# A Fourier branch associated the other way, with seven products in both stages, under an attention on one core

## The chip, the cores and the metric

The kernel runs on one core of a Trainium2 chip. The metric is the time of one execution on the device in microseconds. A core has TensorE (matrix products, PE in the profile, with its weight loads as PEld), VectorE (DVE), ScalarE (ACT), GpSimd (POOL) and SyncE (SP), which here issues all transfers from one queue, in order. Each engine works off its own list of instructions in order and waits for others by semaphores.

## What is computed

Two independent branches, whose results stand side by side in the output (2048 rows, 1024 + 1024 columns). All data are float32.

```
# A: attention, 2048 rows, width 1024, 32 heads of 32, one shared key and value head
q = x @ wq;  k = x @ wk;  v = x @ wv
p = softmax(q k^T * 32**-0.5);  a = (p v) @ wo
# B: Fourier mixing of another x (2048 x 1024)
a_ = x @ hid_re^T;  b_ = x @ hid_im^T         # hid: 1024 x 1024
y  = seq_re @ a_ - seq_im @ b_                # seq: 2048 x 2048
out = concat([a, y], axis=-1)
```

## The kernel before

**Precision.** TensorE multiplies in the type fp32r, which keeps fewer bits than float32. So each operand tile is split into a high part (`hi`, a cast to fp32r) and a low part (`lo`, the tile less its high part), and one product of tiles is three matmuls: high x high, high x low, low x high.

**Fills.** All large products (queries, keys and values, both stages of the Fourier branch, the output projection) are written as a list of *groups*. A group makes one 128 x 512 tile of a result in one PSUM bank (`psb`): 8 right tiles of 128 x 512, 2 left tiles that hold four 128 x 128 blocks each, 24 matmuls. One such matmul is called a *fill* here, and `take(n)` puts the next n of the list into TensorE's order. At the end of a group its `post` moves the bank to SBUF and on to DRAM.

**Right and left tiles.** Two lines of preparation, `RL` and `ML`, bring each tile through four steps: `load` (SyncE, into one of three staging buffers), `comb` (GpSimd adds or subtracts a second source, where a tile is a sum), `hi` (a cast, on ScalarE in the first 120 fills, on DVE after that) and `lo` (a subtraction on DVE). A step is put into the program when the position in the list of fills is within a *lead* of the item's due position (`RL`: 40, 40, 14, 8 fills; `ML`: 52, 36, 27, 21). The finished pairs stay in rings (`rp` of 14, `mp` of 4), and a step `hi` waits in the program until the tile that it replaces has had its last use. Partial results come back through `yp` (4 buffers). In the names of the profile, `r` and `m` are staging tiles, `rh`, `rl`, `mh`, `ml` the high and low parts, `y` the partial results, `qh` an evicted tile.

**Attention.** 32 units (4 blocks of 512 queries x 8 groups of four heads). For each unit there are 32 score steps and 32 exponential steps. A score step makes two matmuls (`pss<-kst,qst`), DVE takes the row maximum over 1024 keys (`nm`, TENSOR_REDUCE) and ScalarE the exponential with its row sums (`pss<-pss,nm`). These sums give the normalisation of the softmax, in a few small DVE operations per unit (`lse_1`, `lse_2`, names `mm`, `md`, `l`, `m`) and one transpose (`lse_3`). An exponential step, 44 steps later, makes the transposed scores (two matmuls, `pst`) and ScalarE their exponential into `p`. After every second chunk of 128 keys, `pv` multiplies the probabilities with v: a burst of 16 matmuls of 32 columns each (`psb<-p,v`, four heads side by side), whose result DVE adds to `ov`.

**The order** is written out by hand. A prologue of 44 score steps puts 7 fills behind each; then 1024 steps follow, each with one score step and one exponential step, and `level` spreads the fills that are left: none in the step in which a burst stands, the rest evenly over the three other steps of a block of four. `aside` keeps bursts and transposes six fills away from the edges of a group, so that its PSUM bank has been emptied.

**The Fourier branch** uses `PRODUCTS`, a scheme with seven products of half-size blocks for a two by two block product. Before, stage 1 makes x times the four blocks (real and imaginary part, two column halves) of the hidden matrix in 64 groups, and GpSimd forms the sums of these that the scheme needs. Stage 2 multiplies with the sequence matrices by the seven products: 112 groups, since the contraction of 1024 is cut into two halves that meet in `hs` (ScalarE copies the first half, DVE adds the second). Results of products are added up in DRAM through `y`.

Of the kernel before, what the change touches and what calls it, by code (L numbers as in the profile page):

```python
# [8 lines left out]
F32 = mybir.dt.float32  # L9
# [7 lines left out]
P = 128  # L17
# [3 lines left out]
DH = 32  # L21
# [47 lines left out]
def tile_kernel(ctx: ExitStack, tc, xT, wq, wkv, wo, xbT, wT, cT, out):  # L69
# [19 lines left out]
    xb_d = [[[dram.tile([P, 4, P], F32, name=f"xb_{s}_{q}_{a}") for a in range(2)] for q in range(2)] for s in range(NC)]  # L89
# [14 lines left out]
    NR0, NM0, NY = 3, 3, 4  # L104
    NR, NM = 14, 4
# [5 lines left out]
    op = pool(ctx, "op", 2, side="right")  # L111
    hp = pool(ctx, "hp", 1, side="right")
# [107 lines left out]
    RL = Line(NR0, NR, (40, 40, 14, 8), load_r, nothing, hi_r, lo)  # L220
# [106 lines left out]
    qp = pool(ctx, "qp", 1)  # L327

# [3 lines left out]
    def kv_post(b):  # L332
        cols = slice(b * W, (b + 1) * W)

        def post(ps):
            kv = qp.tile([2 * DH, W], F32, name="kv")
            act.activation(kv, ps[:2 * DH], AF.Copy)
            dve.tensor_copy(kst[0:DH, cols], kv[0:DH])
            kl = qp.tile([DH, W], F32R, name="kl")
# [38 lines left out]
    NAMES = {}  # L378
    for _, nt, _ in PRODUCTS:
        key = tuple(nt)  # L380
        NAMES[key] = [dram.tile([P, W], F32, name=f"r{len(NAMES)}_{s}") for s in range(NC)]

    def stage1():
        seen = []
        for r, e in ((0, 0), (1, 1), (0, 1), (1, 0)):
            ws = [Item([(lambda c=c, r=r, e=e: wT[r, e, c], 1)]) for c in range(ND)]
            sg = -1 if r else 1
            todo = [k for k in NAMES if len(k) == 2 and all(t[:2] in seen + [(r, e)] for t in k)
                    and any(t[:2] == (r, e) for t in k)]
            seen.append((r, e))  # L390
            for s in range(NC):
                if len(seen) > 1:
                    left = [Item(None, pre=lambda q=q, s=s: xb_d[s][q]) for q in range(2)]
                else:
                    left = [Item([(lambda q=q, s=s: xbT[s, :, q * 4:(q + 1) * 4], 1)], save=xb_d[s][q]) for q in range(2)]
                ys = []
                for k in todo:
                    o = next(t for t in k if t[:2] != (r, e))
                    ys.append(Item([(lambda o=o, s=s: single(o[:2])[s], 1)]))

                def post(ps, r=r, e=e, s=s, sg=sg, ys=ys, todo=todo):
                    o = op.tile([P, W], F32, name="qh")
                    act.activation(o, ps, AF.Copy, scale=float(sg))
                    sp.dma_start(single((r, e))[s], o)
                    ready.add((((r, e, 1),), s))
                    for k, y in zip(todo, ys):
                        mine = next(t[2] for t in k if t[:2] == (r, e))
                        other = next(t[2] for t in k if t[:2] != (r, e))
                        if other > 0:
                            (gp.tensor_add if mine > 0 else gp.tensor_sub)(y.y, y.y, o)  # L410
                        else:
                            gp.tensor_sub(y.y, o, y.y)
                        sp.dma_start(NAMES[k][s], y.y)
                        ready.add((k, s))
                yield Group(left, ws, post, ys=ys)

    singles = {}

    def single(k):
        if k not in singles:  # L420
            key = ((k[0], k[1], 1),)
            singles[k] = NAMES[key] if key in NAMES else [dram.tile([P, W], F32, name=f"n{k[0]}{k[1]}_{s}") for s in range(NC)]
        return singles[k]

    for r in range(2):
        for e in range(2):
            single((r, e))

    hs = {}

    def right_of(k, s):
        assert (k, s) in ready
        return NAMES[k][s]

    def stage2():
        seen, total = {}, {}
        for _, _, outs in PRODUCTS:
            for t, e, _ in outs:
                total[t, e] = total.get((t, e), 0) + 1
        for mt, nt, outs in PRODUCTS[1:] + PRODUCTS[:1]:  # L440
            for half in range(2):
                R = [Item([(lambda s=s, nt=nt: right_of(tuple(nt), s), 1)]) for s in range(half * 8, half * 8 + 8)]
                for k in range(8):
                    left = []
                    for q in range(2):
                        s0 = half * 8 + q * 4
                        left.append(Item([(lambda a=a, k=k, s0=s0: cT[a[0], a[1] * 8 + k, :, s0:s0 + 4], a[2]) for a in mt]))
                    if half == 0:
                        def post(ps, k=k):
                            hs[k] = hp.tile([P, W], F32, name=f"h{k}")  # L450
                            act.activation(hs[k], ps, AF.Copy)
                        yield Group(left, R, post)
                        continue
                    ys = []
                    plan = []
                    for t, e, sg in outs:
                        n = seen.get((t, e, k), 0)
                        seen[t, e, k] = n + 1
                        it = None
                        if n:  # L460
                            it = Item([(lambda t=t, e=e, k=k: y_d[t][e][k], 1)])
                            ys.append(it)
                        r0 = (t * 8 + k) * P
                        to = out[r0:r0 + P, D + e * W:D + (e + 1) * W] if n + 1 == total[t, e] else y_d[t][e][k]
                        plan.append((sg, it, to))

                    def post(ps, k=k, plan=plan):
                        h = hs[k]
                        dve.tensor_add(h, h, ps)
                        for sg, it, to in plan:  # L470
                            if it is not None:
                                (gp.tensor_add if sg > 0 else gp.tensor_sub)(it.y, it.y, h)
                                sp.dma_start(to, it.y)
                            elif sg > 0:
                                sp.dma_start(to, h)
                            else:
                                o = op.tile([P, W], F32, name="qh")
                                act.activation(o, h, AF.Copy, scale=-1.0)
                                sp.dma_start(to, o)
                    yield Group(left, R, post, ys=ys)  # L480
# [286 lines left out]
```

## Time and profile before

| | us |
|---|---|
| median of 3 runs | 2922.26 (2920.36 to 2922.76) |
| span of the profiled execution | 2920.7 |
| TensorE busy | 2870.4 (98%) |
| DVE busy | 2078.9 (71%) |
| ScalarE busy | 2295.2 (79%) |
| GpSimd busy | 465.0 (16%) |
| transfers | 485.05 MB, mean 166 GB/s |

Busy times are unions of the instructions of an engine. Matmuls overlap in the pipeline, so a TensorE that is always busy may still have gaps between starts. In a row for a group of instructions stand, after the shapes and the count, the busy time in us and the mean duration in ns, and behind the second bar the idle time of the engine before them and what ended it. In a row in order of time stand the start and the duration in us. `L50` is the line of the helper class that records all operations, so the names of the tiles tell the operations apart.

### The profile page before, as it was taken

How to read it: one execution, taken by the hardware profiler on the slowest of the kernel's cores; microseconds unless marked ns; L12 is line 12 of the kernel's file. 1: busy time of each engine (PE TensorE's matmuls, PEld its weight loads, DVE VectorE, ACT ScalarE, POOL GpSimd, SP SyncE). 2: the span in 40 equal slices, each digit the busy share in tenths (PEclk: the TensorE clock that was granted, in tenths of full speed). 3: DMA queues.
4: the chain of work that ended last, by engine and by line, in shares of the span. 5: the costliest groups of instructions: out<-in, count | busy, mean ns of one | idle time of the engine just before them, and what ended most of it. 6: DMA issues, size and time to landing. Idle time of an engine off the chain costs nothing.

```text
span 2920.7 us, 40174 instructions
## 1 busy us (share of the span) xinstructions
PE 2870.4 (98%) x14096; PEld 1943.3 (67%) x14096; DVE 2078.9 (71%) x2721; ACT 2295.2 (79%) x3342; POOL 465.0 (16%) x342
## 2 busy tenths in 40 slices
PE   7999999999999999999999999999999999999999
PEld 4776666666666666666666666666666666666666
DVE  6866777655665656888888888788888888866511
ACT  4688888888888887888888888878878888888751
POOL 0000000011112222322233230023232220110000
PEclk9999999999999999999999999999999999999999
DMA  8865455555666666444455463254454442454446
GB/s 279 298 192 171 157 184 172 167 170 185 192 222 216 205 219 220 148 142 147 129 163 170 120 188 116 76 180 141 144 151 134 148 131 80 146 162 136 124 143 178
DMA packets 318027, 485.05 MB, mean 166 GB/s; under 512 B 33664, under 2 KB 98688, under 8 KB 317824
## 3 DMA queue, kind: packets, MB, share of 16 engines
q1 hardware_dynamic: 317824, 482.48, 52.7%
q8 instruction: 111, 1.82, 0.3%
q14 instruction: 92, 0.75, 0.1%
HBM read 351.54 MB, written 129.76 MB: 165 GB/s over the span
## 4 chain that ended last, share of the span: by engine, by line
PE 89%; DVE 4%; ACT 3%; DMA 2%; issue 2%; POOL 0%; SPq 0%; ACTq 0%; POOLq 0%; DVEq 0%
PE psb L50 56%; PE pss L50 16%; PE pst L50 16%; ACT p L50 2%; DVE nm L50 1%; DVE ov L50 1%; DVE rl L50 1%; DVE ml L50 1%; ACT pss L50 0%; DMA ql<-ql 0%; DMA p<-in_xT_dram 0%; DMA r<-in_xT_dram 0%; DVE mh L50 0%; SPq L50 0%; DVE rh L50 0%
## 5 line engine op out<-in xcount | busy, mean ns | idle before, releaser
L50 DVE TENSOR_REDUCE nm<-pss 128x1 f32<-128x1024 f32 x1024 | 1251.0, 1222 | 372.1 <-PE pss L50 366.3
L50 ACT ACTIVATE p<-pst 128x1024 f32<-128x1024 f32 x1024 | 1051.7, 1027 | 407.2 <-PE pst L50 403.4
L50 ACT ACTIVATE pss<-pss,nm 128x1024 f32<-128x1024 f32 x1024 | 1113.8, 1088 | 93.0 <-DVE nm L50 90.6
L50 PE MATMUL psb<-rh,mh 128*128 128x512 f32 (+1 forms) x1916 | 755.3, 394 | 9.6 <-ACT rh L50 6.7
L50 PE MATMUL psb<-rh,ml 128*128 128x512 f32 (+1 forms) x1916 | 755.2, 394 | 0.5 <-DVE ml L50 0.5
L50 PE MATMUL psb<-rl,mh 128*128 128x512 f32 (+1 forms) x1916 | 754.4, 394 | 0.0
L50 PE MATMUL pss<-kst,qst 128*128 128x512 f32 x2048 | 669.4, 408 | 6.9 <-ACT pss L50 6.5
L50 PE MATMUL pst<-qst,kst 128*128 128x512 f32 x2048 | 656.3, 401 | 15.5 <-ACT p L50 15.4
L50 PEld LDWEIGHTS pss<-kst,qst 128*128 128x128 f32 x2048 | 364.3, 188 | 285.2 <-ACT p L50 114.0
L50 PE MATMUL psb<-p,v 128*32 128x512 f32 x4096 | 492.5, 598 | 0.0
L50 PEld LDWEIGHTS pst<-qst,kst 128*128 128x128 f32 x2048 | 373.0, 188 | 141.8 <-ACT p L50 58.5
L50 PEld LDWEIGHTS psb<-rh,mh 128*128 128x128 f32 (+1 forms) x1916 | 359.2, 187 | 96.3 <-ACT rh L50 7.3
L50 PEld LDWEIGHTS psb<-rh,ml 128*128 128x128 f32 (+1 forms) x1916 | 359.2, 187 | 86.8 <-DVE ml L50 1.6
L50 PEld LDWEIGHTS psb<-rl,mh 128*128 128x128 f32 (+1 forms) x1916 | 359.3, 188 | 86.1 <-issue 1.0
L50 DVE TENSOR_TENSOR ov<-ov,psb 128x512 f32<-128x512 f32 x224 | 154.0, 688 | 321.9 <-PE psb L50 321.5
L50 POOL TENSOR_TENSOR m<-m,m 128x512 f32<-128x512 f32 x160 | 216.6, 1360 | 462.7 <-DMA m<-in_cT_dram 352.6
L50 PEld LDWEIGHTS psb<-p,v 128*32 128x32 f32 x4096 | 106.8, 109 | 245.4 <-issue 220.9
L50 ACT ACTIVATION_READ_ACCUMULATOR pss<-pss,nm 128x1 f32 x1024 | 209.7, 205 | 0.0
L50 DVE TENSOR_TENSOR ml<-m,mh 128x512 fp32r<-128x512 f32 (+1 forms) x274 | 202.3, 739 | 4.2 <-ACT mh L50 3.5
L50 POOL TENSOR_TENSOR y<-y,h 128x512 f32<-128x512 f32 x64 | 88.8, 1398 | 564.7 <-DVE h L50 480.3
L50 DVE TENSOR_TENSOR rl<-r,rh 128x512 fp32r<-128x512 f32 x200 | 150.3, 753 | 5.2 <-ACT rh L50 3.9
L50 POOL MEMSET qst<- 32x2048 f32 x32 | 58.5, 1832 | 578.8 <-PE pst L50 547.3
(63 smaller groups left out, 783.6 us busy)
## 6 DMA issues: line engine op xcount, KB each, us to landing
m<-in_cT_dram SPq DMA_DIRECT2D x384, 256.0 KB, 3.7
r<-r SPq DMA_DIRECT2D x112, 256.0 KB, 3.7
mh<-xb SPq DMA_DIRECT2D x96, 256.0 KB, 3.9
ml<-xb SPq DMA_DIRECT2D x96, 256.0 KB, 4.1
y<-y SPq DMA_DIRECT2D x96, 256.0 KB, 2.9
y<-r SPq DMA_DIRECT2D x80, 256.0 KB, 3.1
r<-y SPq DMA_DIRECT2D x80, 256.0 KB, 2.0
qst<-qh SPq DMA_DIRECT2D x64, 256.0 KB, 5.7
```

The lines of the kernel that those rows point to most:

```text
L50: return lambda *a, **k: self.tc.keep_in_program_order(f(*a, **k))
```

## The change

The Fourier branch is associated the other way: stage A multiplies the sequence matrices with x, stage B the result with the hidden matrices. In both, the seven products of `PRODUCTS` are used with a contraction of 1024, so each product tile is one group: stage A has 7 x 2 (real, imaginary) x 2 (column halves of the sequence block) x 4 = 112 groups, stage B 7 x 2 x 4 = 56. The halves and `hs` go.

Stage A takes x in another layout (`xn_d`). It is made in the prologue: `load_x` loads a tile, `turn_x` transposes four 128 x 128 blocks on TensorE per score step (steps 4 to 35), ScalarE copies them out of PSUM, SyncE stores them.

Right tiles can now be sums of two sources too (`load_r` and `comb` on `RL`). The low parts are made on GpSimd after the first 120 fills. Evictions of both stages are on DVE (`evict`), the additions into partial results on GpSimd (`gather`). The tiles of the sequence matrices and the intermediate results are read in pieces of 512 bytes.

The bursts of `pv` take four chunks of 128 keys instead of two: half as many, twice as long, one in eight steps; `level` spreads the fills over the other seven. Buffers: `NY` 3 instead of 4, `NR` 13 instead of 14, `NM` 10 instead of 4, `op` 3 instead of 2, `pp` 5 instead of 4; `hp` and `qp` go. The leads of `RL` are 44, 32, 22, 12. Twenty tiles, not 24, are loaded ahead of everything.

```diff
-    NR0, NM0, NY = 3, 3, 4
-    NR, NM = 14, 4
+    NR0, NM0, NY = 3, 3, 3
+    NR, NM = 13, 10
...
     def load_r(it):
         if it.pre or it.t:
             return
-        it.t = [r0p.tile([P, W], F32, name="r0")]
-        sp.dma_start(it.t[0], it.srcs[0][0]())
+        it.t = []
+        for n, (ap, _) in enumerate(it.srcs):
+            it.t.append(r0p.tile([P, W], F32, name=f"r{n}", bufs=NR0 - n))
+            a = ap()
+            t = it.t[-1]
+            sp.dma_start(t.rearrange("p (a b) -> p a b", a=a.shape[1]) if len(a.shape) == 3 else t, a)
...
     def lo(it):
         if not it.pre:
-            dve.tensor_sub(it.lo, it.t[0], it.hi.bitcast(F32))
+            (dve if pos["fill"] < START else gp).tensor_sub(it.lo, it.t[0], it.hi.bitcast(F32))
...
-    RL = Line(NR0, NR, (40, 40, 14, 8), load_r, nothing, hi_r, lo)
+    RL = Line(NR0, NR, (44, 32, 22, 12), load_r, comb, hi_r, lo)
...
+    ORDER_A, ORDER_B = (2, 4, 1, 5, 0, 3, 6), (0, 4, 1, 2, 3, 5, 6)
...
+    def gather(plan, h):
+        for sg, it, to in plan:
+            if it is None:
+                assert sg > 0
+                sp.dma_start(to, h)
+            else:
+                (gp.tensor_add if sg > 0 else gp.tensor_sub)(it.y, it.y, h)
+                sp.dma_start(to, it.y)
+
+    def evict(ps, sg=1):
+        h = op.tile([P, W], F32, name="qh")
+        if sg > 0:
+            dve.tensor_copy(h, ps)
+        else:
+            dve.tensor_scalar_mul(h, ps, -1.0)
+        return h
+
+    def c_tile(r, c, t):
+        return cT[r, t * 4:t * 4 + 4, :, c].rearrange("t p c -> p t c")
+
+    def stage_a():
+        seen = {}
+        for at, bt, outs in (PRODUCTS[p] for p in ORDER_A):
+            left = [[Item([(lambda i=i, k=k, m=m, q=q: xn_d[i][m][k * 2 + q], sg) for k, i, sg in at]) for q in range(2)]
+                    for m in range(4)]
+            for r in range(2):
+                for t in range(2):
+                    R = [Item([(lambda k=k, j=j, r=r, t=t, c=c: c_tile(r, k * 8 + c, j * 2 + t), sg) for k, j, sg in bt])
+                         for c in range(8)]
+                    for m in range(4):
...
+                        def post(ps, r=r, plan=plan):
+                            gather(plan, evict(ps, -1 if r else 1))
+                        yield Group(left[m], R, post, ys=ys)
...
+    def stage_b():
+        seen = {}
+        for at, bt, outs in (PRODUCTS[p] for p in ORDER_B):
+            R = [Item([(lambda k=k, j=j, c=c: wT[c // 4, j, k * 4 + c % 4], sg) for k, j, sg in bt]) for c in range(8)]
+            for t in range(2):
+                for m in range(4):
                     left = []
+                    for r in range(2):
+                        left.append(Item([(lambda i=i, k=k, r=r, t=t, m=m: gd[k][i][r][t][:, :, m * P:(m + 1) * P].rearrange("i p c -> p i c"), sg)
+                                          for k, i, sg in at]))
...
+                    def post(ps, plan=plan):
+                        gather(plan, evict(ps))
                     yield Group(left, R, post, ys=ys)
...
-    pp = pool(ctx, "pp", 4)
+    pp = pool(ctx, "pp", 5)
...
-        for c in (2 * k, 2 * k + 1):
+        for c in range(4 * k, 4 * k + 4):
             for h in range(4):
-                te.matmul(ps[h * DH:(h + 1) * DH], v[:, c], pt[u, c][:, h], start=c == 2 * k, stop=c == 2 * k + 1)
+                te.matmul(ps[h * DH:(h + 1) * DH], v[:, c], pt[u, c][:, h], start=c == 4 * k, stop=c == 4 * k + 3)
...
+    def turn_x(n, q):
+        i, m = divmod(n, 4)
+        aside()
+        ps = bank("psb")
+        for c in range(4):
+            te.transpose(ps[:, c * P:(c + 1) * P], xt[n][:, q, c * P:(c + 1) * P], ident)
+        o = op.tile([P, W], F32, name="qh")
+        act.activation(o, ps, AF.Copy)
+        cur["at"] += 1
+        sp.dma_start(xn_d[i][m][q], o.rearrange("p (a b) -> p a b", a=4))
+
     for s in range(SU + LEAD):
         score_step(s)
+        if s % 4 == 0 and s < 32:
+            load_x(s // 4)
+        if 4 <= s < 36:
+            turn_x(*divmod(s - 4, 4))
         take(7)
...
-        x = (n // 4 + max(n % 4 - 1, 0) / 3) / (total // 4)
+        x = (n // 8 + max(n % 8 - 1, 0) / 7) / (total // 8)
...
-        if r % 4 == 0 and n:
-            pv(*divmod(n // 4 - 1, 8))
+        if r % 8 == 0 and n:
+            pv(*divmod(n // 8 - 1, 4))
```

More of the change, by code (lines that the diff above doesn't have):

```diff
@@ L375, in q_group @@
         return Group(left, xs, post)
[L378 to L436, printed above, removed]
-        for _, _, outs in PRODUCTS:
[L438 to L443, printed above, removed]
-                    left = []
[L445 to L458, printed above, removed]
@@ new lines, in tile_kernel, with totals @@
+    ORDER_A, ORDER_B = (2, 4, 1, 5, 0, 3, 6), (0, 4, 1, 2, 3, 5, 6)
+    def totals():
+        total = {}
+        for _, _, outs in PRODUCTS:
+            for i, j, _ in outs:
+                total[i, j] = total.get((i, j), 0) + 1
+        return total
+    def gather(plan, h):
[6 more added lines that the diff above has]
+                sp.dma_start(to, it.y)
```

68 lines of the change are left out of this document (38 added, 30 removed).

## Prediction

> **What bounds the kernel now.** I read the page first (busy shares, then the chain), then the table by stretches, then the order of time of a few microseconds in the middle, and last the groups.
>
> ```profile
> span 2920.7 us, 40174 instructions
> ...
> PE 2870.4 (98%) x14096; PEld 1943.3 (67%) x14096; DVE 2078.9 (71%) x2721; ACT 2295.2 (79%) x3342; POOL 465.0 (16%) x342
> ...
> PE 89%; DVE 4%; ACT 3%; DMA 2%; issue 2%; POOL 0%; SPq 0%; ACTq 0%; POOLq 0%; DVEq 0%
> ```
>
> TensorE is busy for 98% and makes 89% of the chain. A busy TensorE is not yet a full one, so I look at the stretches: prologue, query products, the two spectral stages, the output products. The columns are PE, PEld, DVE, ACT, POOL busy, the clock, the DMA share and GB/s.
>
> ```profile
> 120.00:165.00 45.00, 44.96 (x195) 35.83 (x193) 36.23 (x50) 29.17 (x50) 0.00 (x0) 1.00 0.82 271
> 165.00:600.00 435.00, 432.64 (x2151) 292.10 (x2151) 305.07 (x396) 366.33 (x538) 11.09 (x7) 1.00 0.53 171
> 600.00:1100.00 500.00, 496.28 (x2468) 334.80 (x2467) 300.93 (x348) 418.43 (x614) 93.64 (x71) 1.00 0.63 203
> 1100.00:2100.00 1000.00, 987.04 (x4890) 662.70 (x4888) 818.16 (x1091) 819.29 (x1189) 240.50 (x175) 1.00 0.48 148
> ```
>
> TensorE idles for 13 us of 1000 where DVE is 82% busy, for 2.4 of 435 where DVE is 70% busy. The granted clock is 1.00. What one matmul costs is the distance of starts, not its 0.39 us:
>
> ```profile
> 1502.35 0.40 PE L50 MATMUL psb<-rh,ml 128*128 128x512 f32 x1
> 1502.59 0.39 PE L50 MATMUL psb<-rh,mh 128*128 128x512 f32 x1
> 1502.82 0.39 PE L50 MATMUL psb<-rl,mh 128*128 128x512 f32 x1
> 1503.04 0.39 PE L50 MATMUL psb<-rh,ml 128*128 128x512 f32 x1
> 1503.36 1.92 PE L50 MATMUL psb<-p,v 128*32 128x512 f32 x16
> 1505.21 0.73 PE L50 MATMUL pss<-kst,qst 128*128 128x512 f32 x2
> ...
> 1507.39 0.63 PE L50 MATMUL pss<-kst,qst 128*128 128x512 f32 x2
> ```
>
> A fill matmul (one of the 24 of a product) takes 0.23 us, back to back. So the kernel is bound by TensorE's stream of instructions, and I sum over that stream; the other engines count where they make it wait.
>
> **The change, part by part.**
>
> *Fewer products.* Before, the spectral branch has 64 groups (stage 1) and 112 (stage 2: seven products, two halves of the contraction, eight rows of tiles); after, 112 (stage A: 7 products x 2 parts x 2 halves x 4 tiles) and 56 (stage B: 7 x 2 x 4). Eight groups of 24 matmuls go: 192 x 0.23 = 44 us. All of it is on the path.
>
> *Bursts of four chunks.* A burst costs, by the rows above, 0.32 us from the last fill to its first matmul, 1.85 to the next score, and a pair of scores that lasts 0.73 instead of 0.63; less the 0.23 that a fill has anyway, 0.32 + 1.85 + 0.10 - 0.23 = 2.04 us. Doubling it adds four quads of heads. Their weight loads inside the burst show the pace:
>
> ```profile
> L50 PE MATMUL psb<-p,v 128*32 128x512 f32 x4096 | 492.5, 598 | 0.0
> ...
> 1503.82 0.13 PEld L50 LDWEIGHTS psb<-p,v 128*32 128x32 f32 x4 [0.30 <-issue]
> 1504.24 0.13 PEld L50 LDWEIGHTS psb<-p,v 128*32 128x32 f32 x4 [0.30 <-issue]
> ```
>
> 0.42 to 0.43 us a quad, 1.72 for four; by the burst's length (1.92 less one matmul's 0.60, over three) it is 0.44, 1.76. One merged pair saves 2.04 - 1.72 = 0.32 us (0.28 by the other), and 256 bursts become 128: 41 us (36 to 41). It also takes 128 of these additions from DVE, 88 us:
>
> ```profile
> L50 DVE TENSOR_TENSOR ov<-ov,psb 128x512 f32<-128x512 f32 x224 | 154.0, 688 | 321.9 <-PE psb L50 321.5
> ```
>
> The order gets lumpier: no fills in the step with a burst, 38.7 fills over the other seven, so 4 x 0.23 + 5.5 x 0.23 = 2.2 us for such a step instead of 0.92 + 6.7 x 0.23 = 2.5. (38.7 is 228 groups of 24 less the 494 fills of start and prologue and the last 24, over 128 bursts.) ScalarE needs 2.00 us for a step, back to back from 1507.81 to 1509.81, so it still fits:
>
> ```profile
> 1507.81 1.08 ACT L50 ACTIVATE pss<-pss,nm 128x1024 f32<-128x1024 f32 x1
> 1508.81 0.20 ACT L50 ACTIVATION_READ_ACCUMULATOR pss<-pss,nm 128x1 f32 x1
> 1508.90 1.03 ACT L50 ACTIVATE p<-pst 128x1024 f32<-128x1024 f32 x1
> 1509.81 1.09 ACT L50 ACTIVATE pss<-pss,nm 128x1024 f32<-128x1024 f32 x1
> ```
>
> *The transposes of x.* 32 blocks of four are added in the prologue's steps 4 to 35, where TensorE has no idle time (44.96 of 45.00), so they count in full. The nearest rows are the four small transposes of v:
>
> ```profile
> 18.89 0.40 PE L50 MATMUL psb<-rl,mh 128*64 128x512 f32 x1
> 19.82 0.43 PE L50 MATMUL pss<-ident,kv 64*128 64x64 f32 x4 [0.53 <-ACT kv L50]
> 20.18 0.44 PE L50 MATMUL psb<-rh,ml 128*64 128x512 f32 x1
> ```
>
> Without the wait a block adds 0.93 - 0.53 + 0.36 - 0.23 = 0.53 us; these stream 64 columns, the new ones 128, so up to twice the inner 0.36: 0.89. I take 0.66, nearer the row: 32 x 0.66 = 21 us (17 to 28). Their eviction is on ScalarE, which has 16 us of 45 free there.
>
> *Their transfers.* How fast loads go shows at the start, where the queue is full:
>
> ```profile
> 11.02 5.07 SPq L50 DMA_DIRECT2D h<-in_xT_dram  x8
> ```
>
> Eight of 256 KB, one per 0.68 us: 388 GB/s. 32 loads and 32 stores of 256 KB, 16.8 MB, join the prologue's 271 GB/s. Thirty-six steps of 0.46 + 1.61 + 0.66 = 2.7 us make 98 us, with some 21 MB of the query products' own: 38 MB, 385 GB/s. The start's rate is just enough, for pieces of 2 KB; the new loads have 512-byte pieces. So between 0 and 20 us; I take 8, since leads of 30 to 50 fills cover most of it.
>
> *The start.* 20 tiles are loaded ahead instead of 24; four of x go through the three staging buffers, behind SyncE's waits for the keys. Before, such loads came at 21.43 us, after the key moves, and TensorE then stood for 3.90 us:
>
> ```profile
> 20.15 0.60 SPq L50 DMA_DIRECT2D kst<-kst  x1
> ...
> 21.43 4.79 SPq L50 DMA_DIRECT2D r<-in_xT_dram  x4
> ...
> 29.82 0.69 PE L50 MATMUL pss<-ident,kv 64*128 64x64 f32 x4 [3.90 <-ACT kv L50]
> ```
>
> Zero to one more such gap: 0 to 8 us, 4 taken.
>
> *Low parts and sums on GpSimd, evictions on DVE.* The rows that price it:
>
> ```profile
> L50 DVE TENSOR_REDUCE nm<-pss 128x1 f32<-128x1024 f32 x1024 | 1251.0, 1222 | 372.1 <-PE pss L50 366.3
> ...
> L50 POOL TENSOR_TENSOR m<-m,m 128x512 f32<-128x512 f32 x160 | 216.6, 1360 | 462.7 <-DMA m<-in_cT_dram 352.6
> ...
> L50 DVE TENSOR_TENSOR ml<-m,mh 128x512 fp32r<-128x512 f32 (+1 forms) x274 | 202.3, 739 | 4.2 <-ACT mh L50 3.5
> ...
> L50 DVE CAST mh<-m 128x512 fp32r<-128x512 f32 x267 | 130.1, 487 | 13.9 <-POOL m L50 6.9 <-DMA m<-in_wq_dram 5.2 <-PE psb L50 1.4
> ```
>
> From the diff: stages A and B bring 448 new right and left tiles (280 and 168), 320 of them a sum of two sources, and 192 additions into partial results. GpSimd's instructions there are 320 + 448 + 192 = 960 x 1.36 = 1306 us of the two stages' 168 x 12.4 = 2080 us (a group: 24 x 0.23, 4.96 steps of 0.92, 0.62 bursts of 3.76). It goes from 24% to 63% busy. DVE, per group: 4.96 row maxima 6.06, casts 2.5 (A) or 3 (B) at 0.42 undisturbed, eviction 0.69 (as the additions from PSUM above), burst sums 0.43, the softmax's small ones about 0.5: 8.8 to 9.0 us of 12.4, 71 to 73% instead of 82%. So both have room on average. ScalarE loses 128 copies. What is new is that they meet. The two engines hold each other up already:
>
> ```profile
> 1385.07 1.81 POOL L50 MEMSET qst<- 32x2048 f32 x1
> ...
> 1386.08 1.08 DVE L50 CAST mh<-m 128x512 fp32r<-128x512 f32 x1
> ...
> 1392.81 0.42 DVE L50 CAST mh<-m 128x512 fp32r<-128x512 f32 x1
> ...
> 1390.94 0.68 DVE L50 TENSOR_TENSOR ml<-m,mh 128x512 fp32r<-128x512 f32 x1
> 1390.99 1.78 POOL L50 TENSOR_TENSOR m<-m,m 128x512 f32<-128x512 f32 x1 [4.11 <-DMA m<-in_cT_dram]
> ```
>
> The cast that falls into a GpSimd instruction ends only after it, 1.08 instead of 0.42 us; the GpSimd addition begun just after a subtraction takes 1.78. The Trainium skill, page "SBUF — State Buffer", section "Who interferes with whom", says why: casts and two-input operations of VectorE share a port pair with GpSimd, whoever comes second stands until the first is done, and reductions never do. The trace agrees (the row maximum's mean of 1222 ns shows no wait). By that rule at its worst, each of the 4.2 such operations a group behind a whole instruction of 1.36, DVE would need 14.6 of 12.4 us and the sum would be near 3260; by the casts' mean it stays at 2890.
>
> The casts' mean wait is 487 - 420 = 0.07 us at 24% GpSimd; scaled to 63%, 0.18, and for arrivals at random 0.63 x 0.68 (half an instruction) = 0.43 us. With 3.9 to 4.4 such operations a group (casts, and nine a unit in the softmax) DVE needs 0.7 to 1.9 us more, 77 to 88% of the time. From 70 to 82% TensorE's idle rose by 7 in 1000, so I take 10 in 1000 of 2080 us: 20 us. Bounds: 0, and one wait like that cast's, 1.08 - 0.42 = 0.66 us, on the path of each of the 168 groups, 111 us. Queues: GpSimd's additions now wait for DVE's eviction, with combines and low parts queued behind; SyncE's stores wait for these additions, with the next loads queued behind; the lead of 44 or 52 fills (20 us or more) covers that. If this cover goes, it costs TensorE's wait for the low part.
>
> *The sum,* against the profiled 2920.7: -44 - 41 + 21 + 8 + 4 + 20 = -32, 2889 us. The median of the runs, 2922.26, lies 1.6 above that span; I say 2890.
>
> **The rivals.** *All covers hold:* no waits from the ports, the start or the prologue's transfers: 2922 - 44 - 41 + 17 = 2854. For it speaks that DVE is relieved of low parts (the left tiles' alone 202 us); against, that the seven steps between bursts are shorter, 2.2 us.
>
> *The port wait eats it (slower).* Place: DVE in stages A and B, where each cast and two-input operation stands behind a GpSimd instruction, the row maximum behind it is late, and with it the exponential whose bank the next scores need. TensorE then stops. It decides once these waits cost TensorE 52 us, 0.3 us a group; at the bound of 0.66 it is 2922 - 44 - 41 + 21 + 8 + 4 + 111 = 2981, half way between, at 0.48, 2951. For it: GpSimd's share nearly triples, and its queue is in order behind evictions. Against: GpSimd alone, even at 1.78 us each, is not full (1709 of 2080 us), and late row maxima hardly reach TensorE now:
>
> ```profile
> ACT pss L50 <- DVE nm L50: 90.6, 104, 3.9
> ...
> PE pst L50 <- ACT p L50: 15.4, 50, 0.9
> ```
>
> The exponentials stood 104 times for a row maximum, 90.6 us in all and up to 3.9; TensorE stood 15.4 us for them.
>
> *Gain and waits cancel:* waits of some 50 us: 2916 to 2928.
>
> *The burst's price is no fixed overhead* (the change doesn't do what it says): a wait for the probabilities takes its place, and the 41 us stay: 2931. The bursts in the trace wait for nothing, so this is small.
>
> **How the numbers follow.** Forecast (2868 to 2916) 0.52; all covers hold 0.14; cancel 0.10; port wait or the burst's rival 0.24 (0.20 and 0.04). The measurement tells 0.2%, 6 us, from no change. Faster 0.66, same 0.10, slower 0.24. Range 2855 to 2955: below lies little, above some 0.1 of the slower cases; the likeliest one's own is 2868 to 2916.
>
> **What would show it.** Right: 14032 TensorE instructions; bursts of 32 lasting 3.64; about 1050 GpSimd instructions, 1.4 ms; casts at 0.6 us; TensorE's idle in the two stages about 2%. Wrong: gaps in front of scores or exponentials with a late row maximum, or fills that wait for low parts of GpSimd; a prologue longer by over 40 us.

## The result, and the profile after

The changed kernel takes 2992.82 us (median, 2990.9 to 2996.09) beside 2922.51 us for the kernel before: a ratio of 1.0245, interval 1.0231 to 1.026. It is slower by 70 us where 32 us less were forecast, and lies outside the range. Times below are medians; one of the four executions of the kernel with x handed over turned was in a slower state (3129 us), and its median is 2944.27 us with it and 2942.24 without, so differences against that kernel carry some 2 us.

The head of its profile page and the chain of work that ended last:

```profile
span 2990.8 us, 40720 instructions
...
PE 2853.8 (95%) x14032; PEld 1947.9 (65%) x14032; DVE 1966.3 (66%) x2295; ACT 2232.3 (75%) x3246; POOL 1382.7 (46%) x1056
...
PE 67%; DVE 8%; DMA 8%; POOL 6%; ACT 5%; issue 5%; SPq 1%; POOLq 0%; ACTq 0%; DVEq 0%
```

TensorE has less to do, and so has VectorE, 66% instead of 71%. Yet TensorE's share of the chain fell from 89% to 67%; what came in are VectorE, GpSimd, ScalarE and transfers. The stretches say where (columns as in the prediction: PE, PEld, DVE, ACT, POOL, clock, DMA share, GB/s):

```profile
100.00:165.00 65.00, 57.02 (x281) 45.17 (x280) 33.27 (x35) 36.87 (x66) 12.89 (x10) 1.00 1.04 347
165.00:215.00 50.00, 42.48 (x187) 32.84 (x186) 28.32 (x37) 28.46 (x50) 6.45 (x5) 0.97 0.87 285
...
600.00:1100.00 500.00, 481.24 (x2378) 325.23 (x2379) 361.06 (x418) 390.46 (x564) 261.62 (x199) 0.99 0.52 154
1100.00:2100.00 1000.00, 960.35 (x4746) 653.85 (x4745) 697.19 (x818) 777.92 (x1124) 528.61 (x403) 0.99 0.52 154
```

In the prologue TensorE was never idle and now loses 8 us of 65, with the transfers at their limit. In the two stages it idles for 4% of the time, where it was 1%. The waits behind that (total in us, times, longest in us), and three groups:

```profile
ACT pss L50 <- DVE nm L50: 231.5, 162, 5.7
...
PEld pss L50 <- ACT pss L50: 88.5, 66, 3.5
...
DVE rh L50 <- POOL r L50: 77.9, 38, 5.8
...
PE pss L50 <- ACT pss L50: 56.7, 42, 3.1
...
DVE mh L50 <- POOL m L50: 26.6, 24, 3.8
```

```profile
L50 DVE TENSOR_REDUCE nm<-pss 128x1 f32<-128x1024 f32 x1024 | 1246.4, 1221 | 405.4 <-PE pss L50 402.3
...
L50 POOL TENSOR_TENSOR y<-y,qh 128x512 f32<-128x512 f32 x192 | 252.5, 1327 | 442.4 <-DVE qh L50 424.4
...
L50 DVE CAST rh<-r 128x512 fp32r<-128x512 f32 x326 | 248.7, 769 | 122.3 <-POOL r L50 77.9
```

ScalarE stands 231.5 us for row maxima (90.6 before), up to 5.7 us at once, and TensorE's scores stand 56.7 us for the exponential that frees their bank. Before, that was little:

```profile
PE pss L50 <- ACT pss L50: 6.5, 8, 2.2
```

A row maximum itself takes as long as ever (1221 ns). In the order of time it comes late because VectorE, ahead of it in its list, casts for 769 ns instead of the 470 of these casts before, and stands 77.9 + 26.6 us for sums from GpSimd. One such chain, in order of time, parts left out:

```profile
1630.34 2.73 POOL L50 TENSOR_TENSOR y<-y,qh 128x512 f32<-128x512 f32 x2 [10.63 <-DVE qh L50]
...
1631.66 1.75 SPq L50 DMA_DIRECT2D gd<-y  x2
1633.51 0.87 SPq L50 DMA_DIRECT2D y<-gd  x2
...
1634.54 0.93 SPq L50 DMA_DIRECT2D r<-in_cT_dram  x2
...
1640.39 1.28 POOL L50 TENSOR_TENSOR r<-r,r 128x512 f32<-128x512 f32 x1 [5.88 <-DMA r<-in_cT_dram]
...
1641.71 1.50 DVE L50 CAST rh<-r 128x512 fp32r<-128x512 f32 x1 [5.75 <-POOL r L50]
...
1643.12 1.21 DVE L50 TENSOR_REDUCE nm<-pss 128x1 f32<-128x1024 f32 x1
...
1644.43 1.09 ACT L50 ACTIVATE pss<-pss,nm 128x1024 f32<-128x1024 f32 x1 [5.72 <-DVE nm L50]
...
1645.69 0.73 PE L50 MATMUL pss<-kst,qst 128*128 128x512 f32 x2 [2.35 <-ACT pss L50]
```

GpSimd stands 10.63 us for an eviction. SyncE, in order, can store only after the addition and issues the next loads behind that. The sum `r<-r,r` then waits for the load, the cast for the sum, the row maximum behind the cast, the exponential for the maximum, and the scores for their bank.

**Where the 70 us are.** From the starts of all TensorE instructions the span is split into the prologue (up to the first exponential `p<-pst`), the loop to the last one, and the tail. The loop is split into its *stream* (each pair of neighbours at the mean undisturbed distance of such a pair in the kernels here, for two fills 0.230 us, bursts with the switch around them) and its *stands*, the rest. This last split is an estimate, good to a few us.

| us | prologue | stream | stands | tail |
|---|---|---|---|---|
| before | 165.2 | 2645 | 51 | 59.5 |
| after | 212.6 | 2550 | 167 | 61.3 |
| difference | +47 | -95 | +116 | +2 |

Eight of the 95 us are 35 fills that only moved into the prologue. Of the stands, what stood between a product and scores grew from 4 to 63 us, what stood between scores and transposed scores from 24 to 49.

Some 20 us of these stands (3 before) are not waits: TensorE runs there at half its clock. In 11 stretches of the loop, 44 us in all (6.8 before), the granted clock is 0.50, and each of them begins within 5 us of the start of a stand of 1.3 to 3.2 us. Fills are then some 0.43 us apart:

```profile
1509.47 0.73 PE L50 MATMUL pss<-kst,qst 128*128 128x512 f32 x2 [2.78 <-ACT pss L50]
...
1511.80 0.63 PE L50 MATMUL psb<-rh,ml 128*128 128x512 f32 x1
1512.23 0.63 PE L50 MATMUL psb<-rh,mh 128*128 128x512 f32 x1
```

```profile
1510.95:1514.37 3.42, 3.42 (x10) 2.64 (x9) 2.17 (x4) 2.58 (x5) 1.14 (x1) 0.50 0.01 2
```

Not every such stand is followed by one: 37 in the loop lasted over 1 us.

### The profile page after: what moved, and what is told of

It reads as the page before. It is cut to its first block, busy times and chain, and to the rows that moved or that the text cites. A ratio compares the mean times of both kernels' runs of the same rounds, so it can differ in the third digit from the quotient of the medians.

```text
span 2990.8 us, 40720 instructions
## 1 busy us (share of the span) xinstructions
PE 2853.8 (95%) x14032; PEld 1947.9 (65%) x14032; DVE 1966.3 (66%) x2295; ACT 2232.3 (75%) x3246; POOL 1382.7 (46%) x1056
## 4 chain that ended last, share of the span: by engine, by line
PE 67%; DVE 8%; DMA 8%; POOL 6%; ACT 5%; issue 5%; SPq 1%; POOLq 0%; ACTq 0%; DVEq 0%
PE psb L50 43%; PE pst L50 13%; PE pss L50 11%; DMA r<-in_cT_dram 3%; DVE nm L50 3%; ACT p L50 2%; POOL rl L50 2%; ACT pss L50 2%; DVE rh L50 2%; POOL r L50 2%; SPq L50 1%; DVE ov L50 1%; DMA r<-in_xT_dram 1%; DVE mh L50 1%; POOL y L50 1%
## 5 line engine op out<-in xcount | busy, mean ns | idle before, releaser
L50 DVE TENSOR_REDUCE nm<-pss 128x1 f32<-128x1024 f32 x1024 | 1246.4, 1221 | 405.4 <-PE pss L50 402.3
L50 ACT ACTIVATE pss<-pss,nm 128x1024 f32<-128x1024 f32 x1024 | 1114.4, 1088 | 240.3 <-DVE nm L50 231.5
L50 PE MATMUL psb<-rh,mh 128*128 128x512 f32 (+1 forms) x1852 | 737.4, 398 | 24.2 <-DVE ql L50 15.5
L50 PE MATMUL psb<-rh,ml 128*128 128x512 f32 (+1 forms) x1852 | 736.1, 397 | 0.3 <-POOL ml L50 0.3
L50 PE MATMUL psb<-rl,mh 128*128 128x512 f32 (+1 forms) x1852 | 735.8, 397 | 0.3 <-DVE rl L50 0.3
L50 PE MATMUL pss<-kst,qst 128*128 128x512 f32 x2048 | 665.0, 406 | 56.8 <-ACT pss L50 56.7
L50 POOL TENSOR_TENSOR rl<-r,rh 128x512 fp32r<-128x512 f32 x326 | 433.4, 1335 | 612.4 <-DVE rh L50 591.3
L50 PE MATMUL psb<-p,v 128*32 128x512 f32 x4096 | 467.0, 596 | 0.5 <-DVE qh L50 0.5
L50 POOL TENSOR_TENSOR y<-y,qh 128x512 f32<-128x512 f32 x192 | 252.5, 1327 | 442.4 <-DVE qh L50 424.4
L50 POOL TENSOR_TENSOR r<-r,r 128x512 f32<-128x512 f32 x200 | 262.7, 1313 | 301.5 <-DMA r<-in_cT_dram 269.3
L50 POOL TENSOR_TENSOR ml<-m,mh 128x512 fp32r<-128x512 f32 x180 | 235.0, 1306 | 204.8 <-DVE mh L50 107.0
L50 DVE CAST rh<-r 128x512 fp32r<-128x512 f32 x326 | 248.7, 769 | 122.3 <-POOL r L50 77.9
L50 DVE TENSOR_TENSOR ov<-ov,psb 128x512 f32<-128x512 f32 x96 | 65.9, 686 | 272.8 <-PE psb L50 272.7
```

Source lines behind the costliest of these rows:

```text
L50: return lambda *a, **k: self.tc.keep_in_program_order(f(*a, **k))
```

## The experiments

Theories: **W**, GpSimd and SyncE stand in order for the eviction, so sums and casts come late; **P**, VectorE's casts stand for what it shares with GpSimd while that works; **G**, GpSimd has too much work; **B**, the long bursts starve ScalarE; **X**, turning x costs the prologue. The kernel before ran beside each (2921.7 to 2923.8).

**Low parts back on VectorE.**

```diff
-            (dve if pos["fill"] < START else gp).tensor_sub(it.lo, it.t[0], it.hi.bitcast(F32))
+            dve.tensor_sub(it.lo, it.t[0], it.hi.bitcast(F32))
```

> The changed kernel (2993 us) with the low parts back on DVE, all else as changed. GpSimd loses 506 subtractions, 668 us; DVE gains some 340. Theory W (DVE stands in its order behind GpSimd's sums, which stand behind late loads): GpSimd's queue is shorter, the sums come earlier, 2935 to 2960. Theory P (the shared port: casts of 0.77 us instead of 0.42): casts fall below 0.55 us and the time to 2940 to 2970. Rival D (DVE is the engine that is short): 3010 or more.

3009.22 us, 1.0292 (1.0277 to 1.0307), 16 slower than the change, within 1 us of what was named for a VectorE short of time. Casts of `rh` fell to 566 ns and VectorE's stands for the sums `r` to 27.3 us, and it was still slower: VectorE's own time counts as well. Low parts on GpSimd are a gain.

**Casts later in RL.** The step `hi` is put closer to its use, so that a late sum finds no cast waiting.

```diff
-    RL = Line(NR0, NR, (44, 32, 22, 12), load_r, comb, hi_r, lo)
+    RL = Line(NR0, NR, (44, 32, 12, 6), load_r, comb, hi_r, lo)
```

> The changed kernel with one line different: the leads of the right tiles 44, 32, 12, 6 instead of 44, 32, 22, 12, so DVE comes to a right tile's cast ten fills later and the sum has more time. No work is moved. W: DVE's wait for GpSimd's sums of right tiles falls from 78 us to under 20, and the time by 30 to 60 us, 2935 to 2963. P: casts and time stay, 2985 to 3000.

3008.68 us, 1.0288 (1.0265 to 1.0311), 16 slower. The stand of `rh` for `r` went from 78 to 45 us, that of `mh` for `m` rose from 27 to 53. W by leads alone fell: the stand moves to the next cast in the list.

**x handed over turned.** `load_x` and `turn_x` go; the host gives x in the layout of `xn_d`.

```diff
-            left = [[Item([(lambda i=i, k=k, m=m, q=q: xn_d[i][m][k * 2 + q], sg) for k, i, sg in at]) for q in range(2)]
+            left = [[Item([(lambda i=i, k=k, m=m, q=q: xn[4 * i + m, k * 2 + q], sg) for k, i, sg in at]) for q in range(2)]
```

> The changed kernel with x handed over in the turned layout: no loads, transposes, copies and stores of x in the prologue. By the sum on record (21 us of transposes, 8 of transfers) 29 us less, 2964. By the trace, where the first exponential starts 47 us later than before the change, 40 to 50 less, 2943 to 2953, with the first exponential at about 168 us. The waits in the main loop stay as they are.

2944.27 us, 1.007 (1.0054 to 1.0087): X is 48 us. The prologue is 165.7 us, as before. Stands 160.

**The same, loads of x kept; then transposes and evictions kept too.** Only the stores are missing in the second; nothing reads what is loaded or turned.

Loads only:

> x is handed over turned for its use, but its unturned columns are still loaded in the opening as in the change (32 loads of 256 KB); they are not turned and not stored, and nothing reads them. Between 2944 (no turning at all) and 2993 (all of it). If the 48 us are the transfers' (loads and stores in about equal parts): 2960 to 2972. If they are TensorE's (transposes and their stands): 2942 to 2950.

Loads, transposes and evictions:

> As the one with the loads alone, and the 128 transposes and their 32 evictions are done too; only the 32 stores of 256 KB are left out (the use reads x handed over turned). If the cost is TensorE's: 2985 to 2993, all of the 48 us there already. If the stores carry a share by the transfers they delay: 2965 to 2980.

2958.66 us (1.0117, 1.0102 to 1.0132) and 2985.85 us (1.0212, 1.019 to 1.0234). By differences: loads 14, TensorE's transposes with their evictions 27, stores 7. The last two carry some 6 us, since the runs of the second kernel lie 14 us apart; the stores are hardly clear of that. The stretch from 100 to 165 us, in the order no turning, loads only, no stores:

```profile
100.00:165.00 65.00, 65.00 (x283) 52.47 (x282) 47.48 (x59) 42.51 (x73) 16.12 (x12) 1.00 0.82 271
```

```profile
100.00:165.00 65.00, 57.64 (x236) 44.28 (x236) 40.05 (x51) 34.86 (x60) 12.18 (x9) 0.97 1.03 331
```

```profile
100.00:165.00 65.00, 57.93 (x288) 46.38 (x287) 33.27 (x36) 39.38 (x69) 13.31 (x10) 1.00 0.93 291
```

The loads alone fill the transfers (share 0.82 to 1.03) and idle TensorE for 7 us in this stretch. The first time lies between the two ranges; the second is inside the range for TensorE alone, but only because the loads are in it. So it is both.

**Bursts of two chunks in the change, and bursts of four in the kernel before.**

```diff
-        for c in range(4 * k, 4 * k + 4):
+        for c in (2 * k, 2 * k + 1):
...
-        if r % 8 == 0 and n:
-            pv(*divmod(n // 8 - 1, 4))
+        if r % 4 == 0 and n:
+            pv(*divmod(n // 4 - 1, 8))
```

Bursts of two in the change:

> The changed kernel with bursts of two chunks again (fills over three steps of four). By the sum on record a merged pair saves 0.32 us, so this should lose 41 us: 3034. Theory B (the longer burst and the shorter steps of 2.2 us make the waits): the waits shrink by as much as the bursts cost or more, 2960 to 3000.

Bursts of four in the kernel before (the reverse edit, with the buffers that it needs):

> The kernel before with the bursts of four chunks alone (five probability buffers; room for the fifth by sharing four small buffers). TensorE's stream is 41 us shorter. Sum on record: 2882. Theory B (a step between bursts has 2.2 us instead of 2.5 and the row maximum has less room to be late): the waits in the loop, 31 us before, rise by 20 to 45 us, 2900 to 2925.

2983.66 us (1.0212, 1.0197 to 1.0227), 9 less than the change; and 2905.63 us (0.9939, 0.9925 to 0.9954), 17 less than before. In the change, shorter bursts lengthen the stream by 43 us, about as forecast, but the stands fall by 46. In the kernel before, long bursts save 43 in the stream, and 21 come back as stands and 6 in the tail. B has a share in both.

**Additions late** (from here on, x is handed over turned). The addition and its store are issued 8 fills after the eviction, so GpSimd and SyncE do not stand for it.

```diff
-                            gather(plan, evict(ps, -1 if r else 1))
+                            h = evict(ps, -1 if r else 1)
+                            later.append((pos["fill"] + 8, lambda: gather(plan, h)))
```

> The changed kernel with x handed over turned (2944 us), and GpSimd's additions into partial results and SyncE's stores put eight fills behind a group's end, so that GpSimd and SyncE no longer stand for the eviction there (GpSimd stood 433 us for it). Theory W (late sums come from that stand): 20 to 40 us less, 2905 to 2925, DVE's wait for the sums of right tiles under 20 us. Otherwise 2940 to 2950.

2912 us, 0.996 (0.9946 to 0.9975): 32 less than with x turned alone.

```profile
L50 POOL TENSOR_TENSOR y<-y,qh 128x512 f32<-128x512 f32 x192 | 257.2, 1351 | 82.5 <-DVE qh L50 75.8
...
L50 DVE CAST rh<-r 128x512 fp32r<-128x512 f32 x326 | 231.6, 716 | 86.6 <-POOL r L50 50.7
```

GpSimd's stand fell from 432.5 to 75.8 us, the stands of TensorE from 160 to 127. W has a share, though VectorE still stands 50.7 us for the sums of right tiles, where under 20 were expected.

**Casts on GpSimd.**

```diff
-            dve.tensor_copy(to, of)
+            gp.tensor_copy(to, of)
```

> The changed kernel with x handed over turned (2944 us), and the casts on GpSimd too, so that DVE neither waits for GpSimd's sums nor meets it at the port with 505 casts. Theory Q (the row maximum is late because casts in front of it stand, for the port or for a sum): the waits in the loop fall from 110 to under 50 us, 2870 to 2895, and ScalarE's wait for row maxima from 215 to under 100. Rival G (GpSimd is then the engine that is short, some 500 more instructions on 1380 us): fills wait for high or low parts, 2960 or more.

2915.16 us, 0.9963 (0.994 to 0.9987): 29 less. The waits for row maxima halved, to 110.2 us, but now a few were long:

```profile
995.87 1.29 POOL L50 TENSOR_TENSOR r<-r,r 128x512 f32<-128x512 f32 x1
996.50 15.02 DVE L50 TENSOR_TENSOR ov<-ov,rb 128x512 f32<-128x512 f32 x1
997.09 0.62 POOL L50 CAST mh<-m 128x512 fp32r<-128x512 f32 x1
...
1009.15 1.27 POOL L50 TENSOR_TENSOR r<-r,r 128x512 f32<-128x512 f32 x1
1010.36 0.62 POOL L50 CAST mh<-m 128x512 fp32r<-128x512 f32 x1
1011.45 1.21 DVE L50 TENSOR_REDUCE nm<-pss 128x1 f32<-128x1024 f32 x1
...
1012.76 1.09 ACT L50 ACTIVATE pss<-pss,nm 128x1024 f32<-128x1024 f32 x1 [13.90 <-DVE nm L50]
```

One product of two SBUF tiles, 0.69 us elsewhere, lasts 15.02 us while GpSimd works without a pause.

**Evictions on ScalarE.**

```diff
-            dve.tensor_copy(h, ps)
+            act.activation(h, ps, AF.Copy)
```

> The changed kernel with x handed over turned (2944 us), and the 168 evictions of the two stages on ScalarE instead of DVE. If plain work on DVE in front of the row maxima makes the waits (168 x 0.69 = 116 us): 10 to 30 us less, 2915 to 2935. If only the stands at casts do: 2940 to 2955, since ScalarE's 84 us more come between the exponentials.

2940.37 us, 1.0062 (1.0047 to 1.0077): 2 to 4 less. The eviction's own time is not the matter.

**Half of GpSimd's work left out.** Additions late; the low parts of tiles that are not kept are replaced by one tile of zeros, and both rings are one buffer shorter.

> x handed over turned, additions eight fills late, and the low parts of all ring items that are not kept for later left out (a tile of zeros is multiplied in their place, so TensorE's work is the same); GpSimd loses some 300 of its 1056 operations, about 0.4 ms; the ring is one buffer shorter on each side. Theory P (VectorE's casts stand for the port while GpSimd works): ScalarE's wait for nm falls under 120 us (181 now) and the time to 2885 to 2900. Theory G (GpSimd itself is short): it falls to 2880 or less and VectorE's wait for r with it. If neither (what is left is bursts and their neighbours): 2905 to 2918.

2927.29 us, 1.0013 (1.0003 to 1.0022): 15 more than with all of it. GpSimd's busy time fell from 1388.6 to 742.6 us, the casts to 582 ns. G does not fit, here and where GpSimd gets more work below and the kernel is faster. P alone does not fit either: GpSimd, early now, stood for evictions again (366.8 us) and VectorE for its sums (103.6 us). The shorter rings may have a part in it, which no run separates.

**Bursts of two, additions late.**

> x handed over turned, additions eight fills late, and bursts of two key chunks again, beside 2912 with bursts of four. Theory B (a burst of 16 products starves ScalarE whatever else is late): the waits fall by some 45 us of the 85 that are left and the stream grows by 41: 2903 to 2915, no difference. Theory W (the long burst's waits come about only where a late sum meets it, and the late additions have gone): the waits fall by 10 to 25 and the stream grows by 41: 2925 to 2945, so merging the bursts is then worth 15 to 30 us, as it was in the kernel before (17 us).

2919.19 us, 0.9988 (0.9979 to 0.9997): 7 more than with bursts of four. Between the two expectations, nearer to B: the stands fell by 36 us, the stream grew by 43.

**VectorE's two-operand work on GpSimd too,** with casts there, with and without late additions. The minimum becomes a reduction, and the softmax's small operations come one to three steps later (the transpose in step 8 instead of 5).

```diff
-            dve.tensor_sub(d[:, j], m, nm[u][:, j])
+            gp.tensor_sub(d[:, j], m, nm[u][:, j])
...
-            ends.append(lambda: dve.tensor_mul(ov[u], ov[u], rb[u]))
+            ends.append(lambda: eng.tensor_mul(ov[u], ov[u], rb[u]))
```

With late additions:

> x handed over turned, additions and their stores issued eight fills late, the casts (rh, mh) on GpSimd, and of VectorE's operations on two SBUF operands all but the first moved to GpSimd too (differences, products and sums of the softmax's corrections, the product of output and reciprocal, its cast and its remainder; the minimum becomes a reduction over one operand). If the in-order stand of GpSimd and SyncE behind the eviction (theory W) and the wait of VectorE's casts for the shared port (theory P) are two separate costs, their gains add: 2944 less 32 (additions late) less 29 (casts on GpSimd) = 2883, and some 10 less where the stands of up to 15.02 us of VectorE's two-operand operations also reached TensorE: 2870 to 2885, ScalarE's wait for nm under 100 us. If both took away the same waits, the better one of the two stays: 2905 to 2915. If GpSimd is now short of time (theory G; some 1.39 + 0.33 ms busy of 2.9 ms), ring items come late and it is 2920 to 2950, with TensorE waiting for rl or rh.

Without:

> As the kernel with x handed over turned and the casts on GpSimd (2915), with VectorE's two-operand operations on SBUF moved to GpSimd as well; the additions stay where they are. If the stands of single two-operand operations (7 of them over 2.5 us, 5.5 to 15.0 us) cost TensorE most of their length beyond the 7 us of ScalarE's lead, it is 2885 to 2905 and no VectorE operation lasts over 3 us. If they were covered, 2910 to 2920. If GpSimd's longer queue makes the low parts late, 2925 or more.

2916.6 us (0.9977, 0.9967 to 0.9987) and 2923.02 us (1.0002, 0.9992 to 1.0011): both miss. The stands between a product and scores were all but gone (3 and 2 us), but the same edit had brought a new one:

```profile
156.58 1.23 DVE L50 TENSOR_REDUCE nm<-pss 128x1 f32<-128x1024 f32 x1 [0.80 <-PE pss L50]
157.72 0.24 DVE L50 RECIPROCAL m<-l 128x16 f32<-128x16 f32 x1
...
158.11 0.27 PE L50 MATMUL psb<-ident,m 128*48 128x128 f32 x1 [1.57 <-DVE m L50]
```

The reciprocal stood directly ahead of the transpose that reads it, behind a row maximum; once a unit TensorE waited for both.

**The reciprocal one step earlier,** directly after the row maximum of the step before the transpose; with late additions, without, and with bursts of two.

```diff
+            elif e == 7:
+                dve.reciprocal(lse[u][0][:, 2], lse[u][1])
             elif e == 8:
```

With late additions:

> As the kernel with casts and two-operand work on GpSimd and late additions (2917), with the reciprocal of the row sums one step of the scores earlier, so that the transpose no longer stands behind it and behind the row maximum ahead of it (50.6 us of transposes there, 16 to 22 us in the others). If that stand was the whole of what ate the gain: 2917 less 30 = 2880 to 2892. If TensorE's time there was covered by something else (a later wait of the exponentials takes its place): 2905 to 2917.

Without:

> The same without the late additions (2923 with the stand of the transpose). If the port is the larger share: 2885 to 2897, within 8 us of the one with late additions, and the waits ahead of scores stay under 5 us. If late sums are a cost of their own (theory W), these come back as waits of products for low parts and casts on GpSimd, and it is 2905 or more.

With late additions and bursts of two:

> As the first, with bursts of two key chunks. Its stream is 41 us longer. If a burst of sixteen products makes ScalarE late whatever else is late (theory B), the waits ahead of exponentials (50 us) fall to about 20 and the time stays within 12 us of the first. If those waits came of the other two causes and are gone with them, it is 25 to 41 us slower than the first.

2879.83 us (0.9854, 0.9838 to 0.987), the fastest kernel here; 2886.5 us (0.9881, 0.9866 to 0.9896); and 2915.87 us (0.998, 0.997 to 0.9989). Of the first, the waits and the chain:

```profile
ACT pss L50 <- DVE nm L50: 24.9, 33, 1.1
```

```profile
PE 81%; POOL 7%; DMA 5%; issue 3%; ACT 2%; SPq 1%; DVE 1%; POOLq 0%; ACTq 0%; DVEq 0%
```

Late additions are now worth 7 us, not 32, though without them GpSimd still stands 204.8 us for evictions: where no row maximum is queued behind the work that waits for GpSimd, a late sum costs little.

The long bursts are worth 36 us here, but not all of that is the bursts' own. With bursts of two the stream takes 43 us more and the stands only 7 less, because a new stand came with them: the transpose in step 8 now stands directly ahead of a burst, and its copy `mt` behind a row maximum. In most units the burst waits for that copy, some 1 us each time and 22 us in all; the fastest kernel has under 1 us there.

```profile
485.23 1.23 DVE L50 TENSOR_REDUCE nm<-pss 128x1 f32<-128x1024 f32 x1 [0.93 <-PE pss L50]
...
486.38 0.27 DVE L50 COPY mt<-psb 48x128 f32<-48x128 f32 x1
...
486.70 1.92 PE L50 MATMUL psb<-p,v 128*32 128x512 f32 x16 [0.93 <-DVE mt L50]
```

Without it the long bursts would be worth some 14 us, an estimate from these two numbers.

**The change as made, VectorE relieved.** x is turned on the chip, additions are not late.

> The change as made, with x turned on the chip and no late additions; VectorE's casts and two-operand operations on SBUF are on GpSimd, with the reciprocal one step earlier. If the turning of x and VectorE's waits are two separate costs, it is 2886.5 + 48 = 2930 to 2940, so that VectorE's waits stand for 53 to 63 us of the 2993 and the turning for 48. If GpSimd's longer work makes the opening worse, 2945 or more.

2917.64 us, 0.9978 (0.9968 to 0.9988): 75 less than the change and 12 less than the lowest that was expected: the 58 us by which the relief brought the kernel with x turned by the host from 2944 to 2886.5 had been taken for all of it. The two costs do not add: beside 2886.5 us, turning x costs 31 us here, not 48.

```profile
PE 2815.0 (97%) x14032; PEld 1948.8 (67%) x14032; DVE 1511.0 (52%) x1505; ACT 2231.8 (77%) x3246; POOL 1758.6 (60%) x1846
```

```profile
ACT pss L50 <- DVE nm L50: 20.3, 19, 8.0
```

| us | prologue | stream | stands | tail |
|---|---|---|---|---|
| x turned by the host | 165.7 | 2558 | 160 | 60.5 |
| the same, additions late | 165.8 | 2558 | 127 | 60.5 |
| fastest (VectorE relieved, additions late) | 166.5 | 2556 | 97 | 60.6 |
| fastest, bursts of two | 162.7 | 2599 | 91 | 59.1 |
| change, VectorE relieved | 215.3 | 2548 | 90 | 60.6 |

## Why the prediction was wrong

*Fewer products and merged bursts, -85:* right as a change of the stream, which shortened by 95 us, 87 without the fills that moved into the prologue. The bursts' part is 43 us by the run with bursts of two. But the sum gave the bursts no stands of their own, and they were worth only 9 us in the change and 17 in the kernel before.

*Transposes, +21 (17 to 28), and start, +4:* the transposes with their evictions cost 27. With x handed over turned the prologue is as long as before, so the start cost nothing.

*Transfers, +8 (0 to 20):* about 21 (loads 14, stores 7). I had seen that the start's rate is just enough and then let the leads cover most of it; the share of 1.04 shows no cover was left. With this the prologue grew by 47 us, which the prediction had named as a sign of being wrong.

*Waits in stages A and B, +20 (0 to 111):* this is the step that failed. The stands grew by 116 us, some 17 of it at half clock after a stand, which the sum did not have. Relieving VectorE takes 75 us off the change (stands 167 to 90), and 58 off the kernel with x turned by the host. The mechanism is the one of the rival that forecast a slower kernel (a late maximum, a late exponential, a bank not free); at its upper bound it gave 2981. Against that rival the prediction held TensorE's wait for `p`, 15.4 us; the row of the bank that the next scores need is `PE pss <- ACT pss`, 6.5 us before and 56.7 after. Three things went wrong in sizing it.

First, the 20 came from mean loads: idle time against VectorE's share. But from 600 to 2600 us VectorE was busy for 72%, less than the 77 to 88% expected, and TensorE idled for 38 in 1000, where about 20 were expected. The prediction's own rows did not bear the line out: with VectorE at 60% (600 to 1100 us) TensorE idled for 7 in 1000, more than the 5 at 70%. What counts is the single stand of up to 5.8 us ahead of a row maximum. The casts' own wait, 0.18 to 0.43 us, was fair: 769 less 420 is 0.35.

Second, the cover. "The lead of 44 or 52 fills covers that" asked whether TensorE would find its tile in time. It did: outside the stretches at half clock, stands between two products are under 1 us in all. But the cast that waits for the late sum stands in VectorE's list, ahead of row maxima that have no such lead. The cost fell on the scores, not on the products.

Third, "so it still fits" for ScalarE in the short steps. It fits only just: by the prediction's own numbers a step of 2.2 us leaves ScalarE 0.2 us to catch up after a late maximum. Of the 43 us that long bursts save in the stream, 21 came back as stands in the kernel before and 46 in the change. That the 0.2 us are the reason is argued, not shown.

What stays open: the wait for what VectorE and GpSimd share, the late sums and VectorE's own time all went at once when the casts and the two-operand work moved. Late additions alone gave 32 us of it, and half of GpSimd's work alone gave nothing, so their shares are not separate numbers here. In the fastest kernel 97 us of stands remain, 55 of them between scores and transposed scores. Six of these, 23 us together, are the same fault again, brought by the relief: ScalarE stands in order for GpSimd's small differences `md`, which lie behind GpSimd's long operations, and the exponentials stand behind that (27.1 us in all, up to 5.9).

```profile
1659.63 0.40 POOL L50 TENSOR_TENSOR md<-mm,nm 128x16 f32<-128x16 f32 x2
...
1660.06 0.23 ACT L50 ACTIVATE md<-md 128x32 f32<-128x32 f32 x1 [5.27 <-POOL md L50]
...
1661.26 1.22 PE L50 MATMUL pst<-qst,kst 128*128 128x512 f32 x2 [4.69 <-ACT p L50]
```

## What to carry to other kernels

Before giving an engine work that waits for another engine, ask what else stands in its list behind that work: a lead protects the tile, not the urgent instruction queued after it. Here, work that waits for GpSimd did better on GpSimd, where the wait is only its own order; but ask as well who reads its result, as ScalarE did here with `md`. And test a saving of the stream (here the merged bursts) in the kernel that it is meant for: 43 us of stream were worth 7, 9 or 17 us, and the 36 measured in the fastest kernel hold 22 us of a stand that only the shorter bursts have there.

## What the runs showed of the hardware

A VectorE operation on two SBUF tiles can be held for many GpSimd instructions, not one. With the casts on GpSimd, seven such operations lasted 5.5 to 15.02 us; the longest began at 996.50 and ended at 1011.52, 0.54 us after the last of fifteen GpSimd instructions in a row. In the change itself none of them and no cast exceeded 2.11 us; there GpSimd's low parts wait for VectorE's casts, so GpSimd pauses, which is the likely reason, though no run tests it. The Trainium skill, page "SBUF — State Buffer", section "Who interferes with whom", says that whoever issues first has the shared ports "for the whole instruction" and the other blocks; the run agrees that the other engine blocks, but the block outlasted the first instruction by fourteen more. Row maxima out of PSUM kept to means of 1220 to 1224 ns in all of these kernels.
